# Expert tiles of 128 slots in fixed buffers, and a data-dependent tail, in a block-sparse attention and routed-experts kernel

## The chip, the cores and the metric

The kernel runs on one core of one Trainium2 chip. The metric is the device time of the whole program in microseconds (us). Below, PE is the matrix engine (TensorE) and PEld its weight loads, DVE is VectorE, ACT is ScalarE, POOL is GpSimd and SP is SyncE, whose queue issues the plain transfers. A "pass" is one recorded matmul: this fp32 program shows two passes, each with a weight load, for every matmul that is written (1216 are recorded for the 608 of the first expert layer), and one pass for a transpose.

## The reference, cut to what matters

Attention over 4 sequences of 768 tokens with 8 heads of 64 gives 3072 rows of 512 numbers. A router picks one of eight experts for each row and a gate; each expert is two matrices:

```python
expert_idx = np.argmax(logits, axis=1)
for e in range(E):
    mask = expert_idx == e
    h = np.maximum(x[mask] @ w1[e], 0.0)          # w1[e]: 512 x 1024
    out[mask] = gate_w[mask, None] * (h @ w2[e])  # w2[e]: 1024 x 512
```

For the given inputs the reference sends 813, 192, 322, 753, 256, 320, 192 and 224 rows to the eight experts. In pieces of 256 rows that is 4+1+2+3+1+2+1+1 = 15 pieces; in pieces of 128 it is 7+2+3+6+2+3+2+2 = 27.

## The kernel before, in words

Three parts follow each other. The **attention** part walks 192 units (a head and 128 of its queries) with `score`, `turn_probs` and `attend`, and ends each sequence with `route`, which stores the rows and their gates in DRAM (`x_dram`) and keeps each row's expert and rank. `dispatch` then turns ranks into slots: the slots of an expert are padded to a multiple of G = 256, `k.slot` holds the row of each slot (row 3072, one past the end, where the slot is empty) and `k.expert` the expert of each tile. The **expert** part runs NG = 19 tiles of 256 slots, the most that any routing can need.

`fetch` (from L350) loads the tile's expert number into a register of SP, starts two weight transfers of 2 MB each from SP (L354 `w1`, L356 `w2`), and gathers the rows, 128 at a time, with an indirect transfer from POOL (L361). `expert_tile` (from L369) turns the rows with eight PE transposes (L375), copies them to `xgt` half on DVE and half on ACT (L378, L379), multiplies by `w1` into `hp` (L386, 256 columns a pass) with a relu on ACT and DVE (L388, L389), multiplies by `w2` into `yp` (L394, 512 columns a pass, twice), scales by the gate on DVE (L397) and scatters with an indirect transfer from POOL (L399) that drops empty slots. The weights have two buffers in rotation, so the tile after the running one is fetched while it runs. PSUM has three large buffers (`big`) and two small ones (`small`) for the whole kernel.

The kernel is written in program order; a scheduler places each engine's instructions by their dependences and sets the semaphores. Engines run their own queues in order.

Of the kernel before, what the change touches and what calls it, by code (L numbers as in the profile page):

```python
# [10 lines left out]
F32 = mybir.dt.float32  # L11
# [65 lines left out]


def build_mask(k):
    """Rows that extend the contraction of q and k: the key's block one-hot against the  # L80
    query block's mask row (0 where it attends, NEG where not)."""
    nc, pool = k.nc, k.setup
    ids = pool.tile([NB, NRAND], I32, name="ids")
    words = dataclasses.replace(k.blocks.tensor, shape=[NB, 2 * NRAND], dtype=I32)
    with nc.allow_non_contiguous_dma(reason="low words of the block numbers"):
        nc.sync.dma_start(out=ids, in_=bass.AP(tensor=words, offset=0, ap=[[2 * NRAND, NB], [2, NRAND]]))
    ids_f = pool.tile([NB, NRAND], F32, name="ids_f")
    nc.vector.tensor_copy(out=ids_f, in_=ids)

    dif = iota(k, "dif", [NB, NB], [[1, NB]], mult=-1)  # L90
    col = iota(k, "col", [NB, NB], [[1, NB]])
    row = iota(k, "row", [NB, NB], [[0, NB]], mult=1)
    m = pool.tile([NB, NB], F32, name="m")
    nc.vector.tensor_tensor(out=m, in0=dif, in1=dif, op=ALU.mult)
    nc.vector.tensor_scalar(out=m, in0=m, scalar1=1.5, scalar2=None, op0=ALU.is_le)
    for val in (0.0, float(NB - 1)):
        for pos in (col, row):
            nc.vector.scalar_tensor_tensor(out=m, in0=pos, scalar=val, in1=m, op0=ALU.is_equal, op1=ALU.max)
    for r in range(NRAND):
        nc.vector.scalar_tensor_tensor(out=m, in0=col, scalar=ids_f[:, r:r + 1], in1=m,  # L100
                                       op0=ALU.is_equal, op1=ALU.max)
# [12 lines left out]
    nc.vector.tensor_copy(out=krow, in_=kr[0:NB, 0:S])  # L114
    qr = k.big.tile([P, 1024], F32, name="qr", tag="big")
    for lo, hi in ((0, 512), (512, S)):
        nc.tensor.matmul(qr[0:NB, lo:hi], lhsT=m, rhs=krow[:, lo:hi], start=True, stop=True)

    k.sides = []
    for i in range(2):  # L120
        side = {}
        for name, rows, copy in (("q", qr[0:NB, 0:S], nc.scalar.copy), ("k", krow, nc.vector.tensor_copy)):
            for h in range(2):
                side[name, h] = k.const.tile([D + NB, S], F32, name=f"{name}{h}_{i}")
                copy(out=side[name, h][D:D + NB, :], in_=rows)
        k.sides.append(side)
# [103 lines left out]


def route(k, b):
    """Expert, gate and rank within the expert for the tokens of one sequence."""
    nc, p, x = k.nc, k.rp, k.x[b]
    nrm = p.tile([P, NC], F32, name="nrm")
    for c in range(NC):
# [53 lines left out]


def dispatch(k):
    """Slots in expert order: the token of each slot (N where none is), the expert of each tile."""
    nc, p = k.nc, k.dp
    cp = k.small.tile([P, 512], F32, name="cp", tag="small")
    nc.tensor.matmul(cp[:, 0:E], lhsT=k.ones, rhs=k.seen[:, NT, :], start=True, stop=True)
# [9 lines left out]
    for step in (1, 2, 4):  # L306
# [2 lines left out]
        nc.vector.tensor_tensor(out=nxt[:, step:E], in0=end[:, step:E], in1=end[:, 0:E - step], op=ALU.add)  # L309
        end = nxt  # L310

    past = p.tile([P, NG, E], F32, name="past")
    nc.vector.tensor_tensor(out=past, in0=k.tile_no.unsqueeze(2).broadcast_to([P, NG, E]),
                            in1=end.unsqueeze(1).broadcast_to([P, NG, E]), op=ALU.is_ge)
# [32 lines left out]
    nc.vector.tensor_scalar(out=k.slot, in0=ps[:, 0:NS], scalar1=float(N), scalar2=None, op0=ALU.add)  # L347


def fetch(k, i):  # L350
    nc = k.nc
    e = nc.values_load(k.expert[0:1, i:i + 1], engines=(mybir.EngineType.SP,), min_val=0, max_val=E - 1)
    w1 = k.wp.tile([P, ND, F], F32, name="w1", tag="w1")
    nc.sync.dma_start(out=w1, in_=k.w1[bass.ds(e, 1), :, :].rearrange("o (c p) f -> p (o c) f", p=P))  # L354
    w2 = k.wp.tile([P, NF, DM], F32, name="w2", tag="w2")
    nc.sync.dma_start(out=w2, in_=k.w2[bass.ds(e, 1), :, :].rearrange("o (c p) m -> p (o c) m", p=P))  # L356
    xs = []
    for s in range(GS):
# [10 lines left out]
def expert_tile(k, i):  # L369
    nc = k.nc  # L370
    w1, w2, xs = k.fetched.pop(i)
    ps = k.big.tile([P, ND, GS, P], F32, name="xg_ps", tag="big")
    for d in range(ND):
        for s in range(GS):
            nc.tensor.transpose(ps[:, d, s, :], xs[s][:, d * P:(d + 1) * P], k.ident)  # L375
    xt = k.mp.tile([P, ND, G], F32, name="xgt", tag="xgt")
    half = ND // 2
    nc.vector.tensor_copy(out=xt[:, 0:half], in_=ps[:, 0:half].rearrange("p d s t -> p d (s t)"))  # L378
    nc.scalar.copy(out=xt[:, half:ND], in_=ps[:, half:ND].rearrange("p d s t -> p d (s t)"))  # L379

    h = k.mp.tile([P, NF, G], F32, name="h", tag="h")
    for f0 in range(0, NF, 4):
        hp = k.big.tile([P, 4, G], F32, name="hp", tag="big")
        for f in range(4):
            for d in range(ND):
                nc.tensor.matmul(hp[:, f, :], lhsT=w1[:, d, (f0 + f) * P:(f0 + f + 1) * P], rhs=xt[:, d, :],  # L386
                                 start=(d == 0), stop=(d == ND - 1))
        nc.scalar.activation(h[:, f0:f0 + 2], hp[:, 0:2], ACT.Relu)  # L388
        nc.vector.tensor_scalar(out=h[:, f0 + 2:f0 + 4], in0=hp[:, 2:4], scalar1=0.0, scalar2=None, op0=ALU.max)  # L389

    for s in range(GS):
        yp = k.small.tile([P, DM], F32, name="yp", tag="small")
        for f in range(NF):
            nc.tensor.matmul(yp, lhsT=h[:, f, s * P:(s + 1) * P], rhs=w2[:, f, :],  # L394
                             start=(f == 0), stop=(f == NF - 1))
        y = k.gp.tile([P, DM], F32, name="y", tag="y")
        nc.vector.tensor_scalar(out=y, in0=yp, scalar1=xs[s][:, DM:XW], scalar2=None, op0=ALU.mult)  # L397
        t = i * GS + s
        nc.gpsimd.indirect_dma_start(  # L399
            out=k.out[:, :], out_offset=bass.IndirectOffsetOnAxis(ap=k.slot[:, t:t + 1], axis=0),  # L400
            in_=y[:, :], in_offset=None, bounds_check=N - 1, oob_is_err=False,
        )


@with_exitstack
def kernel(
# [15 lines left out]
    n.tc, n.nc = tc, tc.nc  # L422
    n.q, n.k, n.v, n.blocks, n.out = q, k, v, sampled_blocks, out
    n.emb, n.tau, n.w1, n.w2 = moe_expert_emb, moe_tau, moe_w1, moe_w2
    n.loaded, n.vs, n.es, n.ets, n.sums, n.x, n.fetched = {}, {}, {}, {}, {}, {}, {}

    n.const = ctx.enter_context(tc.tile_pool(name="const", bufs=1))
    n.big = ctx.enter_context(tc.tile_pool(name="big", bufs=3, space=PSUM))
    n.small = ctx.enter_context(tc.tile_pool(name="small", bufs=2, space=PSUM))
    n.x_dram = tc.dram_tile([N + 1, XW], F32, name="x_dram")  # L430

    pairs, units = B * NPAIR, B * H * NC
    with ExitStack() as attn:
        def pool(name, bufs):
            return attn.enter_context(tc.tile_pool(name=name, bufs=bufs))
# [24 lines left out]

    with tc.tile_pool(name="dp", bufs=1) as n.dp:
        dispatch(n)
    n.wp = ctx.enter_context(tc.tile_pool(name="wp", bufs=2))
    n.gp = ctx.enter_context(tc.tile_pool(name="gp", bufs=4))
    n.mp = ctx.enter_context(tc.tile_pool(name="mp", bufs=2))
    fetch(n, 0)
    for i in range(NG):
        if i + 1 < NG:
            fetch(n, i + 1)
        expert_tile(n, i)  # L470


# [30 lines left out]
```

## Time and profile before

| | us |
|---|---|
| median of 3 runs (1351.52 to 1358.27) | 1352.59 |
| span of the profiled execution | 1351.6 |
| attention and routing, to about | 750 |
| dispatch, first transfers and gathers, to the first expert matmul | 781.3 |
| 19 expert tiles | 561.2 |
| from the last expert matmul to the end | 9.1 |

PE is busy 96% of the span in the page's count; the other compute engines are below 31%. How to read the views: the page's slices show each engine's busy tenths along the span; the windows give sums by stage; the timeline lists one engine's instructions in order, merged where equal ones follow each other; the DMA view counts queues, and the median time from issue to landing.

### The profile page before, as it was taken

Reading aid. Unit: us, or ns where it says so; the run is one execution under the profiler, and the core shown is the slowest. Engines: PE = TensorE matmul, PEld = TensorE weight load, DVE = VectorE, ACT = ScalarE, POOL = GpSimd, SP = SyncE. Lnnn points to the kernel's source line nnn. Section 1 sums busy time; section 2 is a strip of 40 time slices with the busy share of each in tenths; the row PEclk is TensorE's granted clock in tenths of the full one; section 3 lists DMA queues with packets and bytes.
Section 4 is the critical chain, followed back from the end, with each engine's and each line's share of the span. In section 5 each row is a group of like instructions: output and inputs, shape, how many; then the busy total and the mean of one; then the engine's idle time right before and its main releaser. Section 6 shows DMA issues by size and latency. Waiting matters only on the chain. (4 is left out here: it accounts for less than half of the span.)

```text
span 1351.6 us, 16579 instructions
## 1 busy us (share of the span) xinstructions
PE 1293.4 (96%) x6952; PEld 989.1 (73%) x6952; DVE 410.5 (30%) x619; ACT 358.3 (27%) x660; POOL 89.4 (7%) x125
## 2 busy tenths in 40 slices
PE   6999999999999999999999499999999999999997
PEld 4888888888888888888888466666666666666664
DVE  4444453444444444444444401111111111111110
ACT  3444443444434444444444000000000000000000
POOL 1000000000000000000000101111111111111110
PEclk9999998999979999899999589999999999999999
DMA  3010111111011010110000375544544554454420
GB/s 129 24 36 13 36 36 51 33 36 36 24 60 36 24 36 13 36 48 12 1 1 1 122 283 170 201 161 152 192 170 171 177 202 165 145 197 170 148 71 0
DMA packets 49696, 122.24 MB, mean 90 GB/s; under 512 B 3660, under 2 KB 15948, under 8 KB 49110
## 3 DMA queue, kind: packets, MB, share of 16 engines
q1 hardware_dynamic: 43542, 104.89, 22.1%
q0 software_dynamic: 6080, 16.28, 3.4%
q8 instruction: 55, 0.90, 0.3%
q14 instruction: 19, 0.16, 0.0%
HBM read 108.56 MB, written 16.27 MB: 92 GB/s over the span
## 5 line engine op out<-in xcount | busy, mean ns | idle before, releaser
L184 PE MATMUL sc<-k,q 88*128 88x512 f32 (+1 forms) x768 | 294.6, 506 | 0.0
L386 PE MATMUL hp<-xgt,w 128*128 128x256 f32 x1216 | 270.4, 383 | 14.9 <-DVE xgt L378 14.9
L219 PE MATMUL av<-vld,et 128*128 128x64 f32 x2304 | 278.8, 271 | 0.3 <-ACT et L206 0.3
L189 DVE TENSOR_REDUCE nm<-sc 128x1 f32<-128x768 f32 x192 | 183.9, 958 | 296.9 <-PE sc L184 296.6
L219 PEld LDWEIGHTS av<-vld,et 128*128 128x128 f32 x2304 | 272.3, 192 | 0.5 <-ACT et L206 0.5
L386 PEld LDWEIGHTS hp<-xgt,w 128*128 128x128 f32 x1216 | 231.5, 192 | 50.8 <-DVE xgt L378 19.6
L394 PE MATMUL yp<-w,h 128*128 128x512 f32 x608 | 264.0, 592 | 0.0
L191 ACT ACTIVATE e<-sc,nm 128x768 f32<-128x768 f32 x192 | 173.5, 904 | 172.0 <-DVE nm L189 172.0
L394 PEld LDWEIGHTS yp<-w,h 128*128 128x128 f32 x608 | 115.5, 190 | 137.3 <-issue 136.3
L184 PEld LDWEIGHTS sc<-k,q 88*128 88x128 f32 x768 | 133.1, 194 | 92.2 <-issue 92.1
L201 PE MATMUL et_ps<-ident,e 128*128 128x128 f32 x1152 | 161.6, 277 | 0.8 <-ACT e L191 0.8
L206 ACT COPY et<-et_ps 128x768 f32<-128x768 f32 x128 | 101.8, 796 | 208.2 <-PE et_ps L201 208.2
L201 PEld LDWEIGHTS et_ps<-ident,e 128*128 128x128 f32 x1152 | 141.3, 144 | 18.9 <-ACT e L191 1.2
L389 DVE TENSOR_SCALAR h<-hp 128x512 f32<-128x512 f32 x38 | 26.3, 692 | 271.0 <-ACT h L388 271.0
L397 DVE TENSOR_SCALAR y<-yp,xg 128x512 f32<-128x512 f32 x38 | 28.5, 750 | 221.6 <-PE yp L394 221.6
L379 ACT COPY xgt<-xg_ps 128x512 f32<-128x512 f32 x19 | 11.1, 585 | 300.1 <-DVE xgt L378 300.1
L388 ACT ACTIVATE h<-hp 128x512 f32<-128x512 f32 x38 | 22.7, 597 | 248.0 <-PE hp L386 248.0
L399 POOL DMA_INDIRECT out_dram<-y,slot x38 | 38.4, 1011 | 487.5 <-DVE y L397 487.5
L204 DVE COPY et<-et_ps 128x768 f32<-128x768 f32 x64 | 60.7, 948 | 0.7 <-PE et_ps L201 0.7
L239 POOL TENSOR_TENSOR nrm<-nrm,half 128x6 f32<-128x6 f32 x4 | 5.3, 1330 | 684.1 <-ACT sq L238 684.1
L361 POOL DMA_INDIRECT xg<-x_dram,slot x38 | 37.2, 978 | 31.8 <-DVE slot L347 20.5
L191 ACT ACTIVATION_READ_ACCUMULATOR e<-sc,nm 128x1 f32 x192 | 38.1, 199 | 0.0
(114 smaller groups left out, 437.1 us busy)
## 6 DMA issues: line engine op xcount, KB each, us to landing
w<-in_moe_w_dram SPq DMA_DIRECT2D x38, 2048.0 KB, 9.0
x_dram<-x SPq DMA_DIRECT2D x4, 1539.0 KB, 5.8
kld<-in_k_dram SPq DMA_DIRECT2D x16, 384.0 KB, 3.2
qld<-in_q_dram SPq DMA_DIRECT2D x16, 384.0 KB, 3.6
vld<-in_v_dram SPq DMA_DIRECT2D x16, 384.0 KB, 3.2
xg<-x_dram,slot POOLq DMA_INDIRECT x38, 6.7
out_dram<-y,slot POOLq DMA_INDIRECT x38, 2.8
x_dram<-zero SPq DMA_DIRECT2D x1, 2.0 KB
```

What stands on the lines that cost most here:

```text
L184: nc.tensor.matmul(ps[:, lo:hi], lhsT=side["q", hh][:, c * P:(c + 1) * P], rhs=side["k", hh][:, lo:hi], start=True, stop=True)
L189: nc.vector.tensor_reduce(out=nm, in_=ps[:, 0:S], axis=AX.X, op=ALU.max, negate=True)
L191: nc.scalar.activation(e, ps[:, 0:S], ACT.Exp, bias=nm[:, 0:1], scale=1.0, accum_out=k.sums[u // NC][:, c:c + 1])
L201: nc.tensor.transpose(ps[:, c * P:(c + 1) * P], e[:, c * P:(c + 1) * P], k.ident)
L204: nc.vector.tensor_copy(out=et, in_=ps[:, 0:S])
L206: nc.scalar.copy(out=et, in_=ps[:, 0:S])
L219: nc.tensor.matmul(k.av[:, c, :], lhsT=et[:, kc * P:(kc + 1) * P], rhs=v[:, hh, kc, :], start=(kc == 0), stop=(kc == NC - 1))
L361: nc.gpsimd.indirect_dma_start(out=x[:, :], out_offset=None, in_=k.x_dram[:, :], in_offset=bass.IndirectOffsetOnAxis(ap=k.slot[:, t:t + 1] ...
L386: nc.tensor.matmul(hp[:, f, :], lhsT=w1[:, d, (f0 + f) * P:(f0 + f + 1) * P], rhs=xt[:, d, :], start=(d == 0), stop=(d == ND - 1))
L394: nc.tensor.matmul(yp, lhsT=h[:, f, s * P:(s + 1) * P], rhs=w2[:, f, :], start=(f == 0), stop=(f == NF - 1))
L397: nc.vector.tensor_scalar(out=y, in0=yp, scalar1=xs[s][:, DM:XW], scalar2=None, op0=ALU.mult)
L399: nc.gpsimd.indirect_dma_start(out=k.out[:, :], out_offset=bass.IndirectOffsetOnAxis(ap=k.slot[:, t:t + 1], axis=0), in_=y[:, :], in_offse ...
```

## The change

The expert tile becomes 128 slots (G = 128, GS = 1, NG = 31, NS = 31). Buffers of the expert part are no longer rotated by pools: a helper `ring` allocates a fixed set once and takes number i mod n. Weights have three sets, gathered rows and `y` four, all others two; PSUM is closed after `dispatch` and taken anew (`xg_ps` 2 of one bank, `hp` 2 of two banks, `yp` 2 of one: all eight banks). The copy to `xgt` is one DVE instruction (the ACT half is gone), the relu is one ACT and one DVE instruction over half of `hp` each. Fetches run two tiles ahead. Tiles 0 to 23 run always; `dispatch` leaves the number of tiles that the routing needs in `k.used`, and tiles 24 to 30 stand in seven nested conditional blocks, each with the fetch of the tile two later.

```diff
-G = 256
+G = 128
@@ dispatch
+    k.used = k.const.tile([P, 1], I32, name="used")
+    nc.vector.tensor_copy(out=k.used, in_=end[:, E - 1:E])
@@
+def ring(k, name, i, n, pool, shape):
+
+    key = name, i % n
+    if key not in k.rings:
+        k.rings[key] = pool.tile(shape, F32, name=f"{name}_{i % n}")
+    return k.rings[key]
@@ fetch
-    w1 = k.wp.tile([P, ND, F], F32, name="w1", tag="w1")
+    w1 = ring(k, "w1", i, 3, k.wp, [P, ND, F])
...
-        x = k.gp.tile([P, XW], F32, name="xg", tag="xg")
+        x = ring(k, "xg", i, 4, k.wp, [P, XW])
@@ expert_tile
+    ps = ring(k, "xg_ps", i, 2, k.eps, [P, ND, P])
     for d in range(ND):
-        for s in range(GS):
-            nc.tensor.transpose(ps[:, d, s, :], xs[s][:, d * P:(d + 1) * P], k.ident)
+        nc.tensor.transpose(ps[:, d, :], x[:, d * P:(d + 1) * P], k.ident)
...
+    nc.vector.tensor_copy(out=xt, in_=ps)
...
+    for f in range(NF):
+        for d in range(ND):
+            nc.tensor.matmul(hp[:, f, :], lhsT=w1[:, d, f * P:(f + 1) * P], rhs=xt[:, d, :],
+                             start=(d == 0), stop=(d == ND - 1))
+        if f == half - 1:
+            nc.scalar.activation(h[:, 0:half], hp[:, 0:half], ACT.Relu)
+    nc.vector.tensor_scalar(out=h[:, half:NF], in0=hp[:, half:NF], scalar1=0.0, scalar2=None, op0=ALU.max)
...
+    for f in range(NF):
+        nc.tensor.matmul(yp, lhsT=h[:, f, :], rhs=w2[:, f, :], start=(f == 0), stop=(f == NF - 1))
...
@@ the kernel
-    fetch(n, 0)
-    for i in range(NG):
-        if i + 1 < NG:
-            fetch(n, i + 1)
+    psums.close()
...
+    fetch(n, 0)
+    fetch(n, 1)
+    for i in range(N // G):
+        fetch(n, i + 2)
         expert_tile(n, i)
+    used = n.nc.values_load(n.used[0:1, 0:1], min_val=0, max_val=NG)
+    with ExitStack() as more:
+        for i in range(N // G, NG):
+            more.enter_context(tc.If(used > i))
+            if i + 2 < NG:
+                fetch(n, i + 2)
+            expert_tile(n, i)
```

On PE, the expert part of the kernel before begins like this (a row is one written instruction and how often it follows itself; L345 is the last of `dispatch`, `w_5732` and `w_5734` are the first tile's matrices):

```order
L345 MATMUL slot_ps<-val,lane_oh 128x38 x24
L375 MATMUL xg_ps<-ident,xg 128x128 x8
L386 MATMUL hp<-xgt,w_5732 128x256 x32
L394 MATMUL yp<-w_5734,h 128x512 x16
L375 MATMUL xg_ps<-ident,xg 128x128 x8
```

The same place on PE in the changed kernel (`xg_5737`, `xg_5753`, `xg_5769`, `xg_5840` are the four buffers of gathered rows, so those of tiles 0 to 3; `xg_5737` comes again as tile 4's):

```order
L347 MATMUL slot_ps<-val,lane_oh 128x31 x24
L385 MATMUL xg_ps_5771<-ident,xg_5737 128x128 x4
L385 MATMUL xg_ps_5842<-ident,xg_5753 128x128 x4
L385 MATMUL xg_ps_5771<-ident,xg_5769 128x128 x4
L385 MATMUL xg_ps_5842<-ident,xg_5840 128x128 x4
L394 MATMUL hp_5778<-xgt_5776,w_0_5733 128x128 x32
L402 MATMUL yp_5814<-w_0_5735,h_5779 128x512 x8
L394 MATMUL hp_5849<-xgt_5847,w_1_5749 128x128 x32
L402 MATMUL yp_5885<-w_1_5751,h_5850 128x512 x8
L394 MATMUL hp_5778<-xgt_5776,w_2_5765 128x128 x16
L385 MATMUL xg_ps_5771<-ident,xg_5737 128x128 x4
L394 MATMUL hp_5778<-xgt_5776,w_2_5765 128x128 x16
```

The transposes of the first four tiles now stand before the first `hp`, and those of a later tile in the middle of an earlier tile's `hp`; before, each tile's transposes stood between its predecessor's `yp` and its own `hp`.

At the end of the program PE has in the kernel before:

```order
L394 MATMUL yp<-w_7304,h 128x512 x16
L375 MATMUL xg_ps<-ident,xg 128x128 x8
L386 MATMUL hp<-xgt,w_7399 128x256 x32
L394 MATMUL yp<-w_7401,h 128x512 x16
L498 UNCONDITIONAL_BRANCH
```

and in the changed kernel, from the last tile that always runs (number 23) into the first two conditional blocks:

```order
L394 MATMUL hp_5849<-xgt_5847,w_2_5765 128x128 x32
L402 MATMUL yp_5885<-w_2_5767,h_5850 128x512 x8
L478 TENSOR_LOAD used
L479 COMPARE_AND_BRANCH
L385 MATMUL xg_ps_5771<-ident,xg_5737 128x128 x4
L394 MATMUL hp_5778<-xgt_5776,w_0_5733 128x128 x32
L402 MATMUL yp_5814<-w_0_5735,h_5779 128x512 x8
L479 COMPARE_AND_BRANCH
L385 MATMUL xg_ps_5842<-ident,xg_5753 128x128 x4
```

Nothing is moved across a branch: inside the conditional blocks a tile's transposes stand again right before its own `hp`. Every engine has the same seven compare-and-branch instructions and no barrier stands at them.

## Rows read from the trace of the kernel before

**Rows 1.** The page: engine totals, then slices of 1/40 of the span.

```profile
PE 1293.4 (96%) x6952; PEld 989.1 (73%) x6952; DVE 410.5 (30%) x619; ACT 358.3 (27%) x660; POOL 89.4 (7%) x125
...
PE   6999999999999999999999499999999999999997
...
PEclk9999998999979999899999589999999999999999
...
GB/s 129 24 36 13 36 36 51 33 36 36 24 60 36 24 36 13 36 48 12 1 1 1 122 283 170 201 161 152 192 170 171 177 202 165 145 197 170 148 71 0
```

**Rows 2.** Windows: us, busy of PE, PEld, DVE, ACT, POOL, clock, DMA share, GB/s.

```profile
0.00:750.00 750.00, 733.20 (x4927) 612.97 (x4927) 328.21 (x474) 324.53 (x603) 13.79 (x49) 0.97 0.10 33
...
781.30:811.80 30.50, 30.49 (x96) 20.36 (x97) 2.13 (x3) 1.78 (x3) 1.99 (x2) 0.90 0.70 267
811.80:1342.50 530.70, 516.59 (x1873) 343.56 (x1871) 64.35 (x90) 32.02 (x54) 68.58 (x69) 1.00 0.45 159
1342.50:1351.60 9.10, 0.00 (x0) 0.00 (x0) 0.75 (x1) 0.00 (x0) 0.98 (x1) 0.75 0.00 0
```

**Rows 3.** Timeline of PE, one tile: start us, us, engine, line, what, count.

```profile
1047.62 1.04 PE L375 MATMUL xg_ps<-ident,xg 128*128 128x128 f32 x8
1049.44 14.08 PE L386 MATMUL hp<-xgt,w 128*128 128x256 f32 x64 [0.78 <-DVE xgt L378]
1063.36 13.90 PE L394 MATMUL yp<-w,h 128*128 128x512 f32 x32
1077.09 1.04 PE L375 MATMUL xg_ps<-ident,xg 128*128 128x128 f32 x8
```

**Rows 4.** Timeline of two attention units: weight loads and passes of 64 and 128 columns.

```profile
504.58 0.82 PE L201 MATMUL et_ps<-ident,e 128*128 128x128 f32 x6
...
505.13 1.42 PEld L219 LDWEIGHTS av<-vld,et 128*128 128x128 f32 x12
505.24 1.45 PE L219 MATMUL av<-vld,et 128*128 128x64 f32 x12
```

**Rows 5.** The page's groups: count, busy us, mean ns, idle before and releaser.

```profile
L386 PEld LDWEIGHTS hp<-xgt,w 128*128 128x128 f32 x1216 | 231.5, 192 | 50.8 <-DVE xgt L378 19.6
```

**Rows 6.** Timeline of PE, the first tile.

```profile
778.77 1.75 PE L375 MATMUL xg_ps<-ident,xg 128*128 128x128 f32 x7 [0.67 <-DMA xg<-x_dram,slot]
781.31 16.97 PE L386 MATMUL hp<-xgt,w 128*128 128x256 f32 x64 [0.78 <-DVE xgt L378]
```

**Rows 7.** Timeline of POOL, the fourth gather.

```profile
774.16 0.94 POOL L361 DMA_INDIRECT xg<-x_dram,slot  x1 [0.30 <-issue]
```

**Rows 8.** The tile xg in 774 to 775 us: the landing of that gather.

```profile
DMA to landing us min/median/max: 7.4/7.4/7.4
```

**Rows 9.** Waits of SP's queue: us in total, times, longest.

```profile
SPq L354 <- PE slot_ps L345: 5.4, 1, 5.4
```

**Rows 10.** All groups, shapes apart: the longest step of dispatch.

```profile
L331 DVE TENSOR_TENSOR ge<-pos,by_p 128x936 f32<-128x936 f32 x1 | 1.1, 1132 | 0.0
```

**Rows 11.** Timeline of DVE where one tile ends and the next begins.

```profile
1018.35 0.75 DVE L397 TENSOR_SCALAR y<-yp,xg 128x512 f32<-128x512 f32 x1 [6.12 <-PE yp L394]
1019.23 0.69 DVE L378 COPY xgt<-xg_ps 128x512 f32<-128x512 f32 x1
```

**Rows 12.** DMA, 811.8 to 1342.5 us: packets, MB, share; issues, KB, landing.

```profile
q1 hardware_dynamic: 26128, 69.21, 37.1%
q0 software_dynamic: 5520, 14.71, 7.9%
...
w<-in_moe_w_dram SPq DMA_DIRECT2D x33, 2048.0 KB, 8.9
...
xg<-x_dram,slot POOLq DMA_INDIRECT x33, 6.7
```

**Rows 13.** Windows again: the stretch in which transfers queue behind each other.

```profile
772.00:794.00 22.00, 14.89 (x53) 12.25 (x54) 1.38 (x2) 1.18 (x2) 2.49 (x3) 0.65 1.03 391
```

**Rows 14.** The page's queue that loads code: packets, MB, share of 16 engines.

```profile
q8 instruction: 55, 0.90, 0.3%
```

More of the change, by code (lines that the diff above doesn't have):

```diff
@@ L352, in fetch @@
     e = nc.values_load(k.expert[0:1, i:i + 1], engines=(mybir.EngineType.SP,), min_val=0, max_val=E - 1)
-    w1 = k.wp.tile([P, ND, F], F32, name="w1", tag="w1")
+    w1 = ring(k, "w1", i, 3, k.wp, [P, ND, F])
     nc.sync.dma_start(out=w1, in_=k.w1[bass.ds(e, 1), :, :].rearrange("o (c p) f -> p (o c) f", p=P))
-    w2 = k.wp.tile([P, NF, DM], F32, name="w2", tag="w2")
+    w2 = ring(k, "w2", i, 3, k.wp, [P, NF, DM])
     nc.sync.dma_start(out=w2, in_=k.w2[bass.ds(e, 1), :, :].rearrange("o (c p) m -> p (o c) m", p=P))
@@ L371, in expert_tile @@
     w1, w2, xs = k.fetched.pop(i)
-    ps = k.big.tile([P, ND, GS, P], F32, name="xg_ps", tag="big")
+    x = xs[0]
+    ps = ring(k, "xg_ps", i, 2, k.eps, [P, ND, P])
     for d in range(ND):
-        for s in range(GS):
-            nc.tensor.transpose(ps[:, d, s, :], xs[s][:, d * P:(d + 1) * P], k.ident)
[L376 to L402, printed above, removed]
+        nc.tensor.transpose(ps[:, d, :], x[:, d * P:(d + 1) * P], k.ident)
@@ new lines, in expert_tile @@
+    xt = ring(k, "xgt", i, 2, k.wp, [P, ND, P])
+    nc.vector.tensor_copy(out=xt, in_=ps)
+    hp = ring(k, "hp", i, 2, k.eps, [P, NF, P])
+    h = ring(k, "h", i, 2, k.wp, [P, NF, P])
+    half = NF // 2
+    for f in range(NF):
[4 more added lines that the diff above has]
+            nc.scalar.activation(h[:, 0:half], hp[:, 0:half], ACT.Relu)
@@ new lines, in expert_tile @@
+    nc.vector.tensor_scalar(out=h[:, half:NF], in0=hp[:, half:NF], scalar1=0.0, scalar2=None, op0=ALU.max)
+    yp = ring(k, "yp", i, 2, k.eps, [P, DM])
+    for f in range(NF):
+        nc.tensor.matmul(yp, lhsT=h[:, f, :], rhs=w2[:, f, :], start=(f == 0), stop=(f == NF - 1))
+    y = ring(k, "y", i, 4, k.wp, [P, DM])
+    nc.vector.tensor_scalar(out=y, in0=yp, scalar1=x[:, DM:XW], scalar2=None, op0=ALU.mult)
+    nc.gpsimd.indirect_dma_start(
+        out=k.out[:, :], out_offset=bass.IndirectOffsetOnAxis(ap=k.slot[:, i:i + 1], axis=0),
+        in_=y[:, :], in_offset=None, bounds_check=N - 1, oob_is_err=False,
+    )
@@ L424 @@
     n.emb, n.tau, n.w1, n.w2 = moe_expert_emb, moe_tau, moe_w1, moe_w2
-    n.loaded, n.vs, n.es, n.ets, n.sums, n.x, n.fetched = {}, {}, {}, {}, {}, {}, {}
+    n.rings, n.loaded, n.vs, n.es, n.ets, n.sums, n.x, n.fetched = {}, {}, {}, {}, {}, {}, {}, {}
     n.const = ctx.enter_context(tc.tile_pool(name="const", bufs=1))
-    n.big = ctx.enter_context(tc.tile_pool(name="big", bufs=3, space=PSUM))
-    n.small = ctx.enter_context(tc.tile_pool(name="small", bufs=2, space=PSUM))
     n.x_dram = tc.dram_tile([N + 1, XW], F32, name="x_dram")
     pairs, units = B * NPAIR, B * H * NC
+    psums = ctx.enter_context(ExitStack())
+    n.big = psums.enter_context(tc.tile_pool(name="big", bufs=3, space=PSUM))
+    n.small = psums.enter_context(tc.tile_pool(name="small", bufs=2, space=PSUM))
     with ExitStack() as attn:
@@ L462 @@
         dispatch(n)
[L463 to L465 removed]
+    psums.close()
+    n.wp = ctx.enter_context(tc.tile_pool(name="wp", bufs=1))
+    n.eps = ctx.enter_context(tc.tile_pool(name="eps", bufs=1, space=PSUM))
     fetch(n, 0)
[L467 to L469 removed]
+    fetch(n, 1)
+    for i in range(N // G):
+        fetch(n, i + 2)
         expert_tile(n, i)
+    used = n.nc.values_load(n.used[0:1, 0:1], min_val=0, max_val=NG)
[5 more added lines that the diff above has]
+            expert_tile(n, i)
 _INS = ['q', 'k', 'v', 'sampled_blocks', 'moe_expert_emb', 'moe_tau', 'moe_w1', 'moe_w2']
```

## The prediction

> **What bounds the kernel now.** I read the page's slices first, then windows by stage, then the timeline of one tile, then the transfers. The slices show PE in its top tenth nearly everywhere, with the granted clock at full speed but for one dip in the middle [rows 1]. The windows cut the span in three: attention up to 750 us, where PE is busy 733 of 750; a short start of the expert part at a lower clock; and the expert tiles, 516.6 busy of 530.7 us at clock 1.00, where DVE and ACT work for 64 and 32 us and the transfers move 159 GB/s [rows 2]. The change leaves PE's order up to `slot_ps` as it was, so only the expert part can move, and there PE is the bound.
>
> One tile of 256 slots lasts 1077.09 - 1047.62 = 29.47 us: 1.82 from the first transpose to the first `hp`, in which PE waits 0.78 for the copy, 13.92 from `hp` to `yp`, 13.73 for `yp` [rows 3]. 64 `hp` passes in 13.92 are 0.217 each, 32 `yp` passes 0.429. So the cost goes with the columns that stream: 256 cost half of 512. The weight load of 128 columns before each pass is hidden whole.
>
> Nineteen tiles always run. The reference's routing fills 15 of them; the last four hold no row at all, and the 15 are padded to 3840 slots for 3072 rows. In tiles of 128 the same routing needs 27, which are 3456 slots against 4864 computed now.
>
> **The change, part by part.**
>
> *The pass of 128 columns* is the main term, and no fp32 matmul pass of that width is in the trace. By streaming alone it is half of 0.217, 0.109. The load cannot go faster than it does where passes are short: the twelve loads of `av`, with passes of 64 columns, span 1.42 us with 0.192 for the last, so (1.42 - 0.192)/11 = 0.112 apart [rows 4]. Six transposes of 128 columns, each with a load, take 0.82, or (0.82 - 0.28)/5 = 0.108 apart, 0.28 being the last one's own length [rows 4]. All three rows say that load and stream run side by side, so I take the larger, 0.112. The lower bound is 0.109, the upper one a load that is not hidden at all, 0.192 [rows 5].
>
> *A tile of 128 in the always-run loop* is then 64 x 0.112 = 7.17, plus 0.10 for the change from `hp` to `yp` (I allow what exceeds 64 x 0.216 in the 13.92), plus `yp` at half of 13.73 = 6.87: 14.14. Four transposes add 0.44. They stand in the middle of an earlier tile's `hp`, so their copy has half a tile as cover, and the 0.78 wait goes. The next late thing there would be the copy waiting for its buffer, which the tile two before frees at the end of its `hp`, 7 us before it is needed. Sum 14.58 against 29.47 for twice the slots.
>
> *Twenty-four such tiles*: 24 x 14.14 + 20 x 0.44 = 348.2 us (four sets of transposes stand ahead). The first tile runs at the low clock; that cost 16.97 - 14.08 = 2.9 before [rows 3, 6], and I keep it: 351.1.
>
> *The start.* The first `hp` was at 781.31 [rows 6]. It now stands behind the transposes of tiles 0 to 3, so it waits for the fourth gather. Before, that gather was issued at 774.16 and took 7.4 us [rows 7, 8], with weights pouring in as they will now: 781.5. Four transposes at the low clock, 0.25 each by seven in 1.75 [rows 6], bring 782.5, 1.2 later than now. Two more weight transfers are queued behind the first four and take nothing from what tile 0 needs. SP loads one more expert number before its first transfer, about 0.6; it waits 5.4 there [rows 9], which covers it. `dispatch` handles 31 columns in place of 38; its longest step is 1.1 us [rows 10], so a fifth off a few of these is under 1 us. I leave it out.
>
> *Three conditional tiles.* No scheduling crosses a branch, so here the gap between tiles is back. After the last `yp` pass DVE must first make `y` and then copy: in the trace `y` starts 0.2 after the place of the next transposes and takes 0.75, the copy 0.69 [rows 11]. With only four transposes (0.6 to their end) `y` ends last: 0.2 + 0.75 + 0.04 + 0.69 + 0.05 = 1.73. A tile is 1.73 + 14.14 = 15.87, three are 47.6.
>
> *Branches.* PE takes a load of `used` and four compare-and-branch, the last of which leaves. The trace has no conditional branch. Zero is the lower bound, if the branch is worked off while `yp` passes of 0.429 still run; one code block per branch and engine on the path is the upper, 0.3% x 16 x 1351.6 / 55 = 1.2 us each [rows 14], so 5 us, or 10 if each takes two. I take 1, near the zero, as code is loaded without a gap in PE everywhere in these rows. The Trainium skill (Advanced Engine Details and Errata, Control Flow Timing) gives about 108 ns for a compare-and-branch; four would be an estimate of 0.4 us in place of my 1. No run here shows that figure yet.
>
> *The end.* From the last matmul to the end of the span it is 9.1 us now [rows 2]: `y`, scatter, drain, barrier. After the 27th tile each engine jumps over four tiles and sets its semaphores right; POOL does so only when the scatters have landed. I add 2, with bounds 0 and 6. Two fetches (27 and 28) are made for nothing; the last is issued when tile 25's `yp` ends, some 16 us before the end, and a weight transfer lands in 8.9 [rows 12].
>
> *Transfers.* What hides them is PE's time, which halves per tile while the weights of a tile stay 4.2 MB. Over the 530.7 us, the plain queue was busy 37.1% for 33 weight transfers: 5.97 us each, 11.9 a tile. Gathers and scatters took 7.9% for 18 tiles: 2.3 us each, half of it for 128 slots. Together 13.1 us against 14.58 [rows 12]. Where transfers queue up they reach 391 GB/s [rows 13]; 4.7 MB at that rate are 12.0 us. So the cover is there but thin, 1.5 to 2.5 us a tile. Three weight sets let a transfer be late by two tiles, so single late ones cost nothing.
>
> **Sum.** 782.5 + 351.1 + 47.6 + 1 + 9.1 + 2 = 1193.3 us of span. The median of the runs lies 1.0 above the profiled span, so 1194.
>
> **The rivals.**
>
> *Loads not hidden at 128 columns.* Stream and load are now equally long, so any hand-over between them shows; at 256 columns it could not. At the whole load, 0.192 a pass, a tile is 5.1 us longer, 27 tiles 138: 1332. Against it: the 108 ns transposes have just this load and this width [rows 4], though with one pass for each. The Trainium skill (TensorE: Matmul & The Clock Gate, Back-to-back issue gap) speaks for it: a stream of load-and-matmul pairs at 128 columns runs at about 81 ns a matmul, where the matmul alone would take 56. By that ratio a pass here would be an estimate of 0.162 and the sum about 1280; the trace's rows at 64 columns do not agree. Chance 0.06.
>
> *Transfers set the pace.* If gathers, scatters and weights together run no faster than the mean of the first tile's stretch, 267 GB/s [rows 2], a tile takes 4.7/0.267 = 17.7, and 27 of them 84 more: 1278. At 300 GB/s it is 15.7 and 1224. For it: the thin cover. Against it: 391 GB/s over 22 us with gathers among the weights [rows 13]. Chance 0.09.
>
> *Code.* Each branch waits for its code on PE and then on DVE, and so does the jump at the end, at the upper bounds: 9 + 4 more, 1207. Chance 0.08.
>
> *The skip fails.* All 31 tiles run, 4 x 15.87 more: 1258. Chance 0.02; one tile too many by a rounding of `used` would be 1210 and stays in the forecast's tail.
>
> *Slower than before: transfers one after the other.* If each waits for the one before, a tile costs 8.9 + 8.9 + 6.7 = 24.5 us [rows 12], and 27 tiles end the kernel at some 1459. This decides from (1352.6 - 1.0 - 782.5 - 2.9 - 12.1) / 27 = 20.5 us a tile. Against it: the queueing stretch, where they overlap [rows 13]. PE would also idle there and its clock might fall as in the dip [rows 1]. Chance 0.03.
>
> **How the numbers follow.** The forecast, 1186 (passes at 0.109, no charge for branches and jump) to 1212, has 0.72. The code rival lies in it or just above, and the milder half of the transfer rival up to 1230. A range of 1180 to 1232 holds 0.72 + 0.08 and about half of 0.09, some 0.84, less what I may have overlooked in a part no row shows. About 0.5% is what a measurement of this kernel can tell from no change, so faster means under 1345.8: all cases but the last, less a little for whole loads together with slow transfers, 0.96; within 0.5% 0.01; slower 0.03.
>
> **What would show each step.** The changed trace should have `hp` passes 0.11 apart, a period of about 14.6 us in the always-run loop with no idle PE before `hp`, and the first `hp` at about 782.5. Conditional tiles should be 1.3 us longer than the others, 27 `yp` groups should stand on PE, and transfers should be near 325 GB/s without PE waiting for a weight. The forecast is wrong if `hp` passes are over 0.13, if PE waits for weight transfers, if tiles past the 27th appear, or if the gap at the branches is several us.

## The result, and the profile after

The changed kernel takes 1196.32 us, the median of four runs (1193.38 to 1200.93), beside 1355.12 us for the kernel before on the same chip. The ratio is 0.883, with a 95% interval of 0.879 to 0.887. The forecast was 1194 in a range of 1180 to 1232. The profiled execution took 1199.18 us and has a span of 1197.5.

The page of the changed kernel: engine totals, then GB/s in 40 slices. They answer to [rows 1].

```profile
PE 1145.1 (96%) x7244; PEld 913.5 (76%) x7244; DVE 398.9 (33%) x606; ACT 340.9 (28%) x630; POOL 69.9 (6%) x105
...
GB/s 145 27 15 40 27 15 40 78 16 41 27 14 41 53 41 41 27 14 41 53 14 1 1 1 1 124 398 407 356 325 312 318 319 326 315 330 328 306 266 163
```

PE is as full as before and does 148 us less. The transfers of the expert part run at nearly twice the rate: over 300 GB/s in most slices, where it was 140 to 200.

The windows by stage answer to [rows 2]: stretch, its length, busy time of PE, PEld, DVE, ACT and POOL, granted clock, DMA share, GB/s. 793.4 is the first `yp`, 1138.86 the end of the tiles that always run, 1189.26 the last matmul.

```profile
771.20:784.40 13.20, 4.17 (x16) 3.05 (x17) 1.56 (x3) 0.00 (x0) 4.04 (x4) 0.50 0.89 330
784.40:793.40 9.00, 8.19 (x66) 8.00 (x66) 0.00 (x0) 0.60 (x1) 0.00 (x0) 0.91 1.03 405
793.40:1132.00 338.60, 335.88 (x1923) 243.97 (x1922) 47.46 (x68) 13.74 (x23) 44.89 (x45) 1.00 0.93 335
1132.00:1138.86 6.86, 6.86 (x19) 2.99 (x18) 0.69 (x1) 0.00 (x0) 0.00 (x0) 1.00 0.84 311
1138.86:1189.26 50.40, 45.10 (x253) 31.89 (x251) 6.20 (x9) 1.79 (x3) 5.99 (x6) 1.00 0.69 241
1189.26:1197.50 8.24, 0.01 (x1) 0.00 (x0) 0.75 (x1) 0.00 (x0) 1.01 (x1) 0.67 0.07 25
```

In the 338.6 us of the main stretch PE works for 335.9. In the conditional tiles 5.3 of 50.4 us are idle.

The timeline of PE answers to [rows 3] and [rows 6]: start, length, engine, line, what, count, and in brackets the idle time before it with its releaser. First the end of the dispatch, the last transposes ahead of the first tile and the first two tiles, then the steady part, then a conditional tile.

```profile
760.71 10.45 PE L347 MATMUL slot_ps<-val,lane_oh 128*128 128x31 f32 x48 [7.85 <-DVE lane_oh L346]
...
783.52 1.09 PE L385 MATMUL xg_ps<-ident,xg 128*128 128x128 f32 x4 [0.42 <-DMA xg<-x_dram,slot]
784.40 4.48 PE L394 MATMUL hp<-xgt,w 128*128 128x128 f32 x32
789.69 3.84 PE L394 MATMUL hp<-xgt,w 128*128 128x128 f32 x32 [0.81 <-ACT h L397]
793.37 7.03 PE L402 MATMUL yp<-w,h 128*128 128x512 f32 x16
800.24 3.73 PE L394 MATMUL hp<-xgt,w 128*128 128x128 f32 x32
804.66 3.84 PE L394 MATMUL hp<-xgt,w 128*128 128x128 f32 x32 [0.69 <-ACT h L397]
808.33 7.03 PE L402 MATMUL yp<-w,h 128*128 128x512 f32 x16
...
903.88 8.26 PE L394 MATMUL hp<-xgt,w 128*128 128x128 f32 x72
911.97 7.03 PE L402 MATMUL yp<-w,h 128*128 128x512 f32 x16
918.84 2.84 PE L394 MATMUL hp<-xgt,w 128*128 128x128 f32 x24
921.52 0.82 PE L385 MATMUL xg_ps<-ident,xg 128*128 128x128 f32 x6
922.37 3.84 PE L394 MATMUL hp<-xgt,w 128*128 128x128 f32 x32
926.04 7.03 PE L402 MATMUL yp<-w,h 128*128 128x512 f32 x16
...
1155.66 0.60 PE L385 MATMUL xg_ps<-ident,xg 128*128 128x128 f32 x4
1157.26 3.84 PE L394 MATMUL hp<-xgt,w 128*128 128x128 f32 x32 [1.00 <-DVE xgt L387]
1161.84 3.84 PE L394 MATMUL hp<-xgt,w 128*128 128x128 f32 x32 [0.74 <-ACT h L397]
1165.51 7.03 PE L402 MATMUL yp<-w,h 128*128 128x512 f32 x16
1172.38 0.60 PE L385 MATMUL xg_ps<-ident,xg 128*128 128x128 f32 x4
```

32 `hp` passes span 3.73 us, the last of them 0.277 long (the page's mean), so they stand (3.73 - 0.277)/31 = 0.111 apart. A tile runs from 793.37 to 808.33, 14.96 us, where one of twice the slots took 29.47 [rows 3]. And there is a wait that the prediction does not have: the second half of `hp` stands behind `ACT h`, the relu of the first half.

From about 868 us on the periods go 14.07, 14.97 and 14.96 in turn. In the rows from 903.88 on, 72 `hp` passes stand ahead of one `yp` and 56 ahead of the next: the scheduler has put eight passes of a tile before the `yp` of the tile that precedes it, and six transposes stand between the halves. This work fills most of the same wait, so the trace names no releaser there; three tiles still take 44.00 us, 0.65 more than three times the 14.01 of a tile without transposes or waits (e4 below) and twelve transposes of 0.11.

Attention, which the change leaves alone, differs by some microseconds from one execution to the next: over the twelve profiles of this study `slot_ps` starts between 754.2 and 763.9. So traces are compared below from the end of `slot_ps` to the end of the span, called **the expert part**: 582.6 us in the kernel before (769.02 to 1351.6), 426.3 now (771.16 to 1197.5).

### The profile page after: what moved, and what is told of

Read it like the earlier page. It is cut to its first block, busy times and chain, and to the rows that moved or that the text cites. A ratio compares the mean times of both kernels' runs of the same rounds, so it can differ in the third digit from the quotient of the medians.

```text
span 1197.5 us, 17135 instructions
## 1 busy us (share of the span) xinstructions
PE 1145.1 (96%) x7244; PEld 913.5 (76%) x7244; DVE 398.9 (33%) x606; ACT 340.9 (28%) x630; POOL 69.9 (6%) x105
## 4 chain that ended last, share of the span: by engine, by line
PE 90%; issue 4%; DVE 2%; DMA 2%; POOL 1%; ACT 0%; SPq 0%; POOLq 0%; DVEq 0%; ACTq 0%
PE sc L184 22%; PE av L219 21%; PE hp L394 15%; PE yp L402 14%; PE et_ps L201 11%; PE turn L169 4%; PE lg L253 3%; PE slot_ps L347 1%; PE xg_ps L385 1%; DMA xg<-x_dram,slot 1%; DMA out_dram<-y,slot 1%; DMA ids<-in_sampled_blocks_dram 1%; PE xt_ps L248 0%; DVE xt L250 0%; ACT h L397 0%
## 5 line engine op out<-in xcount | busy, mean ns | idle before, releaser
L394 PEld LDWEIGHTS hp<-xgt,w 128*128 128x128 f32 x1728 | 199.7, 192 | 25.2 <-issue 11.0
L394 PE MATMUL hp<-xgt,w 128*128 128x128 f32 x1728 | 204.4, 277 | 8.8 <-ACT h L397 4.6
L402 PE MATMUL yp<-w,h 128*128 128x512 f32 x432 | 189.9, 592 | 0.0
L402 PEld LDWEIGHTS yp<-w,h 128*128 128x128 f32 x432 | 80.0, 190 | 90.4 <-issue 90.4
L397 ACT ACTIVATE h<-hp 128x512 f32<-128x512 f32 x27 | 16.1, 597 | 412.5 <-PE hp L394 412.5
L404 DVE TENSOR_SCALAR y<-yp,xg 128x512 f32<-128x512 f32 x27 | 20.3, 751 | 158.9 <-PE yp L402 158.9
L398 DVE TENSOR_SCALAR h<-hp 128x512 f32<-128x512 f32 x27 | 18.7, 692 | 160.9 <-PE hp L394 160.9
L405 POOL DMA_INDIRECT out_dram<-y,slot x27 | 27.4, 1015 | 354.6 <-DVE y L404 340.2
L174 DVE COPY k<-turn 64x768 f32<-64x768 f32 x32 | 30.2, 945 | 24.3 <-PE turn L169 24.3
L253 PEld LDWEIGHTS lg<-en,xt 128*128 128x128 f32 x192 | 31.8, 258 | 1.8 <-DVE xt L250 1.5
```

The source lines that it names most:

```text
L174: nc.vector.tensor_copy(out=dst[0:D, :], in_=ps[0:D, 0:S])
L253: nc.tensor.matmul(lg[:, c, :], lhsT=xt[:, (c - c2) * ND + d, :], rhs=k.en[:, d, :], start=(d == 0), stop=(d == ND - 1))
L394: nc.tensor.matmul(hp[:, f, :], lhsT=w1[:, d, f * P:(f + 1) * P], rhs=xt[:, d, :], start=(d == 0), stop=(d == ND - 1))
L402: nc.tensor.matmul(yp, lhsT=h[:, f, :], rhs=w2[:, f, :], start=(f == 0), stop=(f == NF - 1))
```

## The experiments

### Where the gain comes from

**e1_skip256** keeps 256 slots and takes the rest of the change: fixed buffers, and conditional blocks from tile 12 on.

```diff
-G = 128
+G = 256
-    w1 = ring(k, "w1", i, 3, k.wp, [P, ND, F])
+    w1 = ring(k, "w1", i, 2, k.wp, [P, ND, F])
```

(`w2` likewise, fetches one tile ahead, and the tile's instructions are those of the kernel before, on rings.)

> Tiles of 256 slots as in the kernel before, in fixed buffers of the same number (two weight sets, fetched one tile ahead), but only 12 tiles always run and tiles 12 to 18 stand in conditional blocks, so that the 15 tiles run that the routing fills. Theory A (PE's passes that are executed are the cost): four tiles of 29.47 us fall away, 118 us, and at most another 0.8 us a tile where the copy's wait is hidden by the fixed buffers: 1223 to 1237. Theory B (the gain comes from the small tiles; skipping empty ones only removes work that was cheap, since their scatters drop every row): within 20 us of the kernel before.

Measured: 1237.49 us, ratio 0.912 (0.910 to 0.915). PE's timeline of its last conditional tiles:

```profile
1166.52 1.04 PE L385 MATMUL xg_ps<-ident,xg 128*128 128x128 f32 x8
1168.34 14.08 PE L396 MATMUL hp<-xgt,w 128*128 128x256 f32 x64 [0.79 <-DVE xgt L388]
1182.26 13.90 PE L404 MATMUL yp<-w,h 128*128 128x512 f32 x32
1195.99 1.04 PE L385 MATMUL xg_ps<-ident,xg 128*128 128x128 f32 x8
```

The period is still 29.47 us, inside conditional blocks too, so neither the fixed buffers nor a branch changes a tile of 256. Fifteen tiles run, and the expert part is 465.2 us: 117.4 less than before, for four tiles of 29.47 = 117.9.

**e2_all31** has tiles of 128 and runs all 31.

```diff
-    for i in range(N // G):
-        fetch(n, i + 2)
+    for i in range(NG):
+        if i + 2 < NG:
+            fetch(n, i + 2)
         expert_tile(n, i)
-    used = n.nc.values_load(n.used[0:1, 0:1], min_val=0, max_val=NG)
-    ...
```

> The changed kernel with all 31 tiles of 128 always run, no conditional block. Theory A: four more tiles of 14.7 us, and the three conditional ones lose what the branches cost them, 3 x 2.0 in the changed kernel's trace: 1196 + 59 - 6 = 1249, and 104 us under the kernel before. Theory C (the empty tiles were what the change removed, small tiles bring nothing): the time of the kernel before, some 1350.

Measured: 1249.01 us, ratio 0.922 (0.919 to 0.924); the expert part is 478.2 us, 104.4 less than before. So the two halves of the change overlap in what they save: dropping empty tiles alone gives 117.4, small tiles alone 104.4, both together 582.6 - 426.3 = 156.3. After the small tiles the skip still brings 51.9; after the skip the small tiles bring 38.9. Both remove padding, and padding goes only once.

**e3_flat27** runs exactly 27 tiles without a conditional block (right for this routing alone).

```diff
-    for i in range(N // G):
-        fetch(n, i + 2)
+    for i in range(27):
+        if i + 2 < 27:
+            fetch(n, i + 2)
         expert_tile(n, i)
-    used = n.nc.values_load(n.used[0:1, 0:1], min_val=0, max_val=NG)
-    ...
```

> The changed kernel with exactly 27 tiles always run and no conditional block (it is right for this routing alone); the two fetches made for nothing are gone too. If the conditional blocks cost only the pipelining that they break, each of the three tiles falls from 16.75 to about 14.7 us and nothing else moves: 6 us less, 1190. If the jump at the end costs as forecast (2 us): 1188. If the branches cost nothing at all: 1196.

Measured: 1195.36 us, ratio 0.881 (0.878 to 0.884), a median that cannot be told from that of the changed kernel: `slot_ps` starts at 763.85 in its trace, 3.1 later. Its expert part is 418.9 us, 7.4 less. Of that 6.2 are the three tiles, at a mean of 14.67 in place of 16.75; 0.8 is the end, 7.4 us after the last matmul in place of 8.2. So conditional execution costs some 7 us, and nearly all of it is that no work is placed across a branch, not the branches (e5 below shows the same).

### The wait that the prediction missed

**e4_split** gives `hp` two tiles of one bank each in place of one tile of two.

```diff
-    hp = ring(k, "hp", i, 2, k.eps, [P, NF, P])
+    hp = [ring(k, f"hp{s}", i, 2, k.eps, [P, NF // 2, P]) for s in range(2)]
-        nc.scalar.activation(h[:, 0:half], hp[:, 0:half], ACT.Relu)
+        nc.scalar.activation(h[:, 0:half], hp[0], ACT.Relu)
```

> The changed kernel with hp as two tiles of one PSUM bank each in place of one of two banks; nothing else. In the changed kernel's trace the second half of the hp passes waits nine times, 5.3 us in all, for ACT to have read the first half. Theory D (the wait is only that two halves of one tile are held for one thing): the waits go, 5 us less, 1191. Theory E (the second half waits for something that lies in the data, or the time is taken up by a later wait): no change, 1196.

Measured: 1195.24 us, ratio 0.880 (0.877 to 0.882). PE's timeline in the steady part:

```profile
1004.83 7.31 PE L394 MATMUL hp<-xgt,w 128*128 128x128 f32 x64
1011.97 7.03 PE L402 MATMUL yp<-w,h 128*128 128x512 f32 x16
1018.84 1.04 PE L385 MATMUL xg_ps<-ident,xg 128*128 128x128 f32 x8
1020.45 7.41 PE L394 MATMUL hp<-xgt,w 128*128 128x128 f32 x64 [0.57 <-DVE xgt L387]
1027.69 7.03 PE L402 MATMUL yp<-w,h 128*128 128x512 f32 x16
```

The 64 passes now run through, and the wait for ACT is gone. So the data did not ask for it: the relu reads the first half while PE would write the second, and the two were ordered only because both halves were one tile. But the transposes were placed anew: those of two tiles stand together between a `yp` and an `hp`, whose copy is then waited for. Periods alternate between 14.01 and 15.72, a mean of 14.76 against 14.72 before the split: in the tiles that always run the time is taken up by a later wait, as theory E has it. The expert part is 423.3 us, 3.0 less, and the median, 1.1 under that of the changed kernel, cannot be told from it; the three conditional tiles, 15.72 to 15.87 in place of 16.72 to 16.80, give the 3.0 alone. The period of 14.01 (here 1004.83 to 1018.84) is worth noting: it is a tile without transposes or waits.

**e5_split_ahead** adds to it that the next tile's transposes and copy are written between the two halves of `hp`, in conditional blocks too.

```diff
         if f == half - 1:
+            if i + 1 < NG:
+                prep(k, i + 1)
             nc.scalar.activation(h[:, 0:half], hp[0], ACT.Relu)
@@ (prep holds the transposes and the copy to xgt; the first call stands before the loop)
+    prep(n, 0)
```

> hp as two tiles of one bank, and the next tile's four transposes and its copy written between the two halves of this tile's hp, in the conditional blocks too (the last of them prepares a tile that is not needed). In the run with the two tiles alone, tiles of 14.01 us alternate with tiles of 15.72, in which the transposes stood before their own hp. If the place of the transposes is all that the waits were exchanged for, every tile, conditional or not, is 14.01 + 0.44 = 14.45, and from the end of slot_ps to the end of the span it takes about 412 us (changed kernel 426.3, two tiles alone 423.3): median 1182 to 1186. If something else keeps PE at 14.7 on average, the time stays at 1195.

Measured: 1185.17 us (median of six, 1177.93 to 1195.59), ratio 0.874 (0.871 to 0.878). PE's timeline from the last tile that always runs into the first conditional ones:

```profile
1123.30 7.03 PE L409 MATMUL yp<-w,h 128*128 128x512 f32 x16
1130.17 3.73 PE L399 MATMUL hp<-xgt,w 128*128 128x128 f32 x32
1133.74 0.60 PE L384 MATMUL xg_ps<-ident,xg 128*128 128x128 f32 x4
1134.18 3.74 PE L399 MATMUL hp<-xgt,w 128*128 128x128 f32 x32
1137.75 7.03 PE L409 MATMUL yp<-w,h 128*128 128x512 f32 x16
```

There is no wait left, and 24 of the 26 periods are 14.45 us, those of the conditional tiles included: 14.01 and 0.44 for four transposes. So the branches themselves cost nothing that this trace shows. The first two, with their transposes elsewhere, are 14.01 and 14.02. The expert part is 412.2 us, 14.1 less than in the changed kernel; the medians differ by 11.2, and the intervals of the two ratios do not overlap. This version beats both kernels. It also says what a wait costs: where the changed kernel's timeline shows 0.69 of idle time, the period is 14.96 - 14.01 = 0.95 longer, since the end of a pass is modelled and the first half-group after a stop spans 3.84 in place of 3.73.

### Whether transfers are the next bound

**e7_two_sets** has two sets of weights in place of three, fetched one tile ahead.

```diff
-    w1 = ring(k, "w1", i, 3, k.wp, [P, ND, F])
+    w1 = ring(k, "w1", i, 2, k.wp, [P, ND, F])
@@ (w2 likewise)
-    fetch(n, 1)
-        fetch(n, i + 2)
+        fetch(n, i + 1)
@@ (and the same in the conditional blocks)
```

> The changed kernel with two weight sets and fetches one tile ahead, as in the kernel before. A set's transfers may start when the tile that used it is through with it and must land one tile (14.6 us) and one layer (7 us) later; one transfer took 10.5 us in the changed kernel. If transfers follow each other without a gap, that is enough and PE waits nowhere: 1196. If two transfers and the rows together need more than the 14.6 us of a tile when they start later, PE waits for a weight in every tile and its clock may fall: 1210 or more.

Measured: 1199.26 us, ratio 0.884 (0.880 to 0.887), and an expert part of 426.7 us against 426.3. The periods are the same 14.96 and 14.07. At this rate the third set brings nothing that can be measured.

**e6_extra_w1** transfers a third 2 MB per tile, which nothing reads.

```diff
+    w3 = ring(k, "w3", i, 3, k.wp, [P, ND, F])
+    nc.sync.dma_start(out=w3, in_=k.w1[bass.ds(e, 1), :, :].rearrange("o (c p) f -> p (o c) f", p=P))
```

> The changed kernel with a third 2 MB transfer a tile (w1 once more, into buffers that nothing reads): 6.3 MB of weights and 0.5 MB of rows a tile. It measures what the transfers can carry beside this PE work. If it is 391 GB/s, as where they queued in the kernel before, a tile takes 17.4 us and 27 tiles make some 70 us more, 1266. If the 335 GB/s of the changed kernel's own always-run loop, at a DMA share of 0.93, is the limit with 7% to spare, so 360, a tile takes 18.9 us and the time is 1305. If transfers are far from their limit, as PE's lack of waits might suggest, nothing changes: 1196.

Measured: 1370.5 us in one run, slower than the kernel before, with periods of 21.5 to 24 us, once 28, up to tile 20. But the transfers' rate was only 323 GB/s, and PE's waits by releaser (total us, times, longest) name another transfer:

```profile
PE xg_ps L387 <- DMA xg<-x_dram,slot: 126.4, 21, 9.9
```

None of the expectations had this. It waits for gathered rows, not for weights: the scheduler had placed the transposes of tile i+4 into the `hp` of tile i+1. Four buffers hold gathered rows, so the gather for these transposes cannot start before `y` of tile i has read its buffer, just ahead. Two causes were mixed, and each got its own run.

**e9_ahead3** has no extra transfer; starting from e5 it writes gathers and transposes three tiles ahead, with the same four buffers.

```diff
-            if i + 1 < NG:
-                prep(k, i + 1)
+            if i + 3 < NG:
+                prep(k, i + 3)
@@ (gathers are written by a function of their own, three tiles ahead; four xgt)
```

> No extra transfer: the kernel with the two hp tiles, but the transposes of a tile stand three tiles ahead of it, in the second half of hp, while the gathered rows keep four buffers. The rows that a transpose needs are then gathered into a buffer that was freed by the y of the tile just before, 4.5 us earlier on PE. Theory F (the run with the third transfer was slow because PE waited for a gather whose chain is y, scatter, gather, landing, 9.7 us from the end of yp, and not because the transfers had no room): the same wait here, 5 us a tile and more where the clock falls after it, 19 to 23 us a tile, 1310 to 1400 in all. Theory G (too many bytes): nothing is added here, so 14.45 us a tile and 1185.

Measured: 1379.25 us in one run. First PE's timeline, then that of POOL, then PE's waits:

```profile
1029.47 7.03 PE L414 MATMUL yp<-w,h 128*128 128x512 f32 x16
1036.34 4.63 PE L404 MATMUL hp<-xgt,w 128*128 128x128 f32 x40
1046.05 1.12 PE L389 MATMUL xg_ps<-ident,xg 128*128 128x128 f32 x4 [5.08 <-DMA xg<-x_dram,slot]
```

```profile
1037.57 1.01 POOL L417 DMA_INDIRECT out_dram<-y,slot  x1 [21.20 <-DVE y L416]
1038.89 0.98 POOL L376 DMA_INDIRECT xg<-x_dram,slot  x1 [0.30 <-issue]
```

```profile
PE xg_ps L389 <- DMA xg<-x_dram,slot: 143.4, 28, 6.3
```

Read as one chain: `yp` ends at 1036.5, `y` follows on DVE, POOL issues the scatter at 1037.57 and behind it the gather at 1038.89, its rows have come at 1046.05, and the transposes that wait for them stand in the middle of the `hp` after that `yp`. That is 9.5 us against 4.6 us of `hp` to cover it. Periods are 20.6 to 23.7 us at 225 GB/s, so the transfers are not what is short. This is the mechanism of e6.

**e11_ahead3_xg8** is e9 with eight buffers of gathered rows.

```diff
-        x = ring(k, "xg", i, 4, k.wp, [P, XW])
+        x = ring(k, "xg", i, 8, k.wp, [P, XW])
```

> The same with eight buffers for gathered rows, so that each gather is issued four tiles earlier. Theory F: the wait is gone, 14.45 us a tile, 1182 to 1186. Theory H (it is the place of the transposes on PE that costs, not the gather): as slow as with four.

Measured: 1215.45 us in one run, 30 more than expected. The tiles that always run are back at 14.45, which settles that the buffers held up the gathers in e9. But the three conditional tiles take 22.75 to 23.79, with waits of 5.9 to 6.4 us for gathered rows: gather and transposes of a tile stand in the same block there, so eight buffers do not take the landing off the path.

**e10_extra_xg6** is e6 with six such buffers, so that the third transfer stands alone.

```diff
+    w3 = ring(k, "w3", i, 3, k.wp, [P, ND, F])
+    nc.sync.dma_start(out=w3, in_=k.w1[bass.ds(e, 1), :, :].rearrange("o (c p) f -> p (o c) f", p=P))
-        x = ring(k, "xg", i, 4, k.wp, [P, XW])
+        x = ring(k, "xg", i, 6, k.wp, [P, XW])
```

> The changed kernel with the third 2 MB transfer a tile again, and six buffers for gathered rows, so that a gather is issued two tiles earlier and no transpose stands close behind it. Theory F: PE waits for no gather; what is left is the transfers' own limit. 29 fetches of 6.3 MB and 27 tiles of 0.5 MB are 197 MB; at 400 GB/s, as in the first 60 us of the changed kernel's always-run loop, they take 492 us, so the kernel ends at about 1265 and a tile takes 17.0 us. If the limit is 360 GB/s: 18.9 us a tile and about 1320. If the bytes were the reason of the slow run: still 22 us a tile, 1370.

Measured: 1265.53 us in one run, as expected at 400 GB/s. A window of 400 us of it, and PE's waits for weights:

```profile
800.00:1200.00 400.00, 360.62 (x2012) 255.99 (x2011) 47.84 (x70) 14.33 (x24) 44.78 (x45) 1.00 1.03 408
```

```profile
PE hp L396 <- DMA w<-in_moe_w_dram: 21.8, 21, 1.7
```

With six buffers PE waits 0.8 us in all for gathered rows, where it was 126 with four (e6). Here the transfers do set the pace, at 408 GB/s, with PE at full clock beside them; periods have a mean of 16.5 us over the always-run tiles. At that rate the 4.7 MB of the changed kernel's tile need 11.5 us of its 14.7: a cover of 3.2 us, not the 1.5 to 2.5 of the prediction. Once the start's backlog is gone the changed kernel runs at 322 GB/s, four fifths of what the transfers can do.

## Why the prediction was right

The sum went from the end of `slot_ps` to the end in 1193.3 - 769.0 = 424.3 us; measured are 426.3. The agreement is partly luck, as errors cancel: -0.3 us for the start, +3.4 for the tiles that always run, +2.8 for the conditional ones, -3.9 for branches and end. Term by term:

- **The pass of 128 columns**: 0.112 forecast, 0.111 measured. Load and stream run side by side at equal length. The rival of loads that are not hidden falls: 0.111 is within 2% of the 0.109 that streaming alone would give. The Trainium skill (TensorE: Matmul & The Clock Gate, Back-to-back issue gap) has a ratio of 81 to 56 at this width, by which the estimate for a pass is 0.162. The trace, at 0.111, does not agree.
- **A tile of 128** without transposes: 14.14 forecast, 14.01 measured (e4, e5); transposes 0.44, exact. Over 27 tiles this is 3.5 us less than forecast.
- **The tiles that always run**: 351.1 forecast, 1138.86 - 784.40 = 354.5 measured. The step that failed is the sentence on "the next late thing": it looked at the buffers of the copy and never at the relu. In the kernel before, `hp` was taken in pieces of four chunks from a rotating pool; now PE's second half and ACT's relu of the first share one tile. The mean period is 14.72 in place of 14.45. Over all 24 tiles, 354.5 less 24 x 14.01, 20 x 0.44 and 0.9 for the low clock leaves 8.6 us for the wait. The trace puts down 3.2 of them to ACT as idle time, in six tiles; that the rest belongs to the same wait is borne out by e5, which is without it and takes 347.3 us for these tiles, 7.2 less, with one set of transposes more. In the conditional tiles it is 3 x (0.74 + 0.27) = 3 more, 0.27 being what a stop costs beyond the idle time shown (e5).
- **The first tile at the low clock**: 2.9 forecast, about 0.9 measured (784.40 to 793.37 is 8.97 us, the same stretch of the next tile 808.33 - 800.24 = 8.09). The granted clock was 0.50 from 771.2 to 784.4 and back at full speed from about 786 on. The first `hp` now stands behind sixteen transposes in place of eight [rows 6], and these ran at the low level in its place; the prediction counted them as time only.
- **The start**: 13.5 us from `slot_ps` to the first `hp` forecast, 784.40 - 771.16 = 13.24 measured. It was read rightly as the fourth gather.
- **Conditional tiles**: 15.87 forecast, 16.80, 16.72 and 16.72 measured. The gap for `y` and copy is 1.60 to 1.68 (forecast 1.73), and the waiting relu adds a full 0.74 of idle time, as no transposes stand between the halves of `hp` there.
- **Branches and end**: 1 + 11.1 forecast. For the branches nothing is measured that can be told from zero: the first conditional tile, with the load of `used` before it, is 0.08 longer than the next two, and in e5 there is no difference. The end is 8.24. The instructions of line 479 by engine, with count, shortest, median and longest in ns, say why:

```profile
L479 PEldq COMPARE_BRANCH  x5: 65/92/3331, 1133.6 to 1189.5; - x5
...
L479 POOLq INC_SWDGE_SEM  x1: 1292/1292/1292, 1190.5 to 1190.5; - x1
```

  PE's branches start while a `yp` still streams: the first at 1133.6, in the `yp` that ends at 1138.86; the one that leaves, of 3331 ns, at 1183.27, in the last `yp`, which ends at 1189.26. So these four lie beside work; the fifth, at 1189.5, is behind the last `yp`, where `y` and the scatter are still to come. Setting POOL's semaphore right took 1.29 us from 1190.5, right behind the issue of the last scatter at 1190.33 and not, as the prediction has it, when the scatters have landed (this one landed after 2.6 us). The whole end is 0.9 shorter than before in place of 2 longer. In e1, the skip with tiles of 256, it is 11.5, 2.4 longer than before; tiles of 128 without the skip end in 8.0 (e2) and 7.4 (e3). So the charge of 2 for the jump is near what 256 slots show, while the smaller tiles' end is shorter; why, no run shows. The Trainium skill (Advanced Engine Details and Errata, Control Flow Timing) gives about 108 ns for a compare-and-branch. Here those that enter a block took 65 and 92 on PE, the one that leaves thirty times as much, and neither sets the time.
- **Transfers**: about 325 GB/s forecast, 322 measured in the steady part, and no wait of PE for a weight: PE's waits name the relu, the copy and, at the start, gathered rows. The mean of the first tile's stretch, on which the rival's 1278 rested, was a start and not a limit: 405 GB/s in that place now.
- **27 tiles** ran; the skip does what it says.

The slower rival, transfers one after the other, did not come. What would have made this kernel slower is another thing that the prediction did not name, shown by e6 and e9: with four buffers of gathered rows, transposes placed three tiles early put the chain from `y` over scatter and gather to landing on PE's path. The order of the changed kernel stays clear of it: tile 4's transposes, the first that reuse a buffer, stand in the `hp` of tile 2, more than a tile of 14.7 us behind the `y` that frees it, and the chain takes 9.5. An edit that touches none of these lines (e6) moved them a tile forward. So the cover is there, but the prediction never worked it out.

## What to carry to other kernels

Padding is counted in slots computed times the pass's price per column, and two edits that both remove padding do not add up. When a tile is halved, look again at every pair of engines that share one buffer in halves: here the passes of two buffers came to fit into one, and a relu of 0.6 us between its halves held PE up for 0.95 us; two buffers in place of two halves take it off (e4, e5). Before a wait is called hidden, follow the transfer behind it to the buffer that it needs, and ask which instruction frees that.

## What the runs showed of the hardware

TensorE's granted clock fell in a wait of 6 us. In e9, PE's stretches around one wait for a gather (columns as in the windows of the result):

```profile
994.50:1000.40 5.90, 0.00 (x1) 0.00 (x0) 0.00 (x0) 0.00 (x0) 0.00 (x0) 0.85 0.84 304
1000.40:1005.90 5.50, 5.49 (x28) 5.49 (x29) 0.69 (x1) 0.00 (x0) 0.00 (x0) 0.54 0.02 3
1005.90:1012.00 6.10, 6.10 (x18) 2.75 (x17) 0.69 (x1) 0.00 (x0) 0.00 (x0) 1.00 0.75 271
```

PE stood still for 5.9 us, then worked 5.5 us at a granted clock of 0.54, nearly the 1.2 GHz level, and was back at 2.4 GHz. 24 `hp` passes took 4.82 us there, 0.20 each, where 40 take 4.63 at full clock. So this wait of 6 us cost some 2 more behind it: 24 passes at 0.111 would have taken 2.7.

Plain transfers with gathers among them reached 401 to 408 GB/s while PE ran at full clock, more than the 391 of [rows 13], and a conditional branch whose engine was still busy with earlier work cost that engine nothing that the trace shows (e5: 14.45 us a tile with branches and without).
